# Dense weights converted in pairs of blocks, with a score tile as the integer scratch

## The chip, the core and the metric

The kernel runs on one core of a Trainium2 chip. The metric is the device time in microseconds from the launch to the end. Before the change it is 780.61 us (median of 3 runs, 776.25 to 781.67). The core's engines work side by side from queues of their own: TensorE (PE, with weight loads as PEld), VectorE (DVE), ScalarE (ACT), GpSimd (POOL), and SyncE (SP), which here only issues DMAs.

## The reference, cut to what matters

```python
# attention: 2 batches x 8 heads, 768 tokens, head size 64; a key counts for a query only in the same bucket
mask = q_bucket[:, :, :, None] == k_bucket[:, :, None, :]        # 6 sign bits of x @ proj
scores = np.where(mask, scale * q @ k.T, -1e9)
attn = softmax(scores); x = attn @ v                             # -> x: 1536 tokens x 512
# dense layer
h = x @ w_in                                                     # w_in 512 x 2048, float64
x = (h * (1 / (1 + np.exp(-1.702 * h)))) @ w_out                 # w_out 2048 x 512, float64
# mixture of 8 experts, the best 2 of a token, chosen by noisy logits
out[mask] += top2_w[mask, k, None] * (np.maximum(x[mask] @ w1[e], 0) @ w2[e])
```

The two dense weights come as float64. [...]

## The kernel before, in words

**Steps of attention.** 96 steps g go over (batch, chunk of 256 queries, pair of heads, head, half of the chunk). A step multiplies 128 queries with all 768 keys (`qk`, L269) into a score tile `s` of 128x1024 float32 in PSUM. The pool `pss` has two such tiles. `rowmax` (L281, DVE) reads the scores, writes them to SBUF as `e` and takes the row maximum; ACT forms the exponential (`expo`, L289 and L290). Steps below 24 transpose `e` on PE (L308), copy it on ACT (L316) and multiply with V in float32 (L376). Later steps split `e` into two float16 halves (`e_hi` L329, `e_lo` L338), transpose by DMA and multiply in float16 (L383). In the loop, step g issues the score product of g+2 first, then the row maximum of g+1, and last the other work due at g. `buckets` writes into the unused columns of a score tile.

**Dense layer.** After every 16 steps a chunk of 256 tokens goes through 16 parts: eight first-layer parts (`h`, L486), then two second-layer results (`px`, L497). Between them a part goes through `th` (L504, L516) and is split into `gt` (L530, L532). Afterwards routing scatters rows to a table in DRAM, and the eight experts run (L864, L895).

**Weights of the dense layer.** They come in 32 blocks of 128x512: 16 of `w_in`, then 16 of `w_out`. `w_load` issues a 512 KB DMA on SP. The raw 4 KB per partition of the first 16 blocks lies in eight regions of the still unused tiles `wo`, those of the others in `wraw`, which has three buffers. `w_bits` makes a float32 from the integer halves with three DVE instructions (L443, L446, L449); their integer tile `pfi` has one bank of PSUM of its own (tag `pb`), which only routing uses later. `w_split` scales on POOL (L462), writes the high half on ACT (L465) and the low half on POOL (L466).

**What sets the order.** PARAM holds due steps: `W` gives the step at which each block is converted, with its load due two steps ahead; `KA`, `QA`, `VA` are those of the stacked keys, queries and values, `PV` of the product with V, `ST` of the start of a chunk's dense part, `RA` of its routing, `O0` and `I0` of the DMAs that clear the output and the table. Strings choose an engine per item (`GS` for the low half of `gt`, `XN` for that of `xt`, `SC` for a scaled copy of `qsa` or `ks`, `HI` for `e_hi`). Emission in this order is a priority: up to the end of attention a scheduler with a cost model of its own fixes the queue of every engine, so instructions of neighbouring steps are interleaved. Once fixed, every engine works its queue in order, and an instruction that waits holds those behind it.

Of the kernel before, what the change touches and what calls it, by code (L numbers as in the profile page):

```python
# [57 lines left out]
PARAM = dict(GM=16, HE=lambda nm, b: 'D', OE=lambda nm, b: 'D', SC=lambda nm, b: 'D', WB=0, XO=lambda b: 'D', NG=16, WS=lambda i: 'P', TS=lambda g: True, XL=lambda g: 'D', GW=2, E0=7, T0=12, T1=16, EL=8, WX=3, PV={(1,2,3):4}, PVD=5, ST={}, VA={}, RA={}, O0=48, OS=2, IS=2, FU=16, VF=2, EC=lambda g: 'AA', QX=8, QS=3, EA=1, S1=(8,8,8,9,9,9,11,13), QE=8, XG=2, XB=2, PC=2, OH=3, BK=3, R0=18, R1=0, LK=8, WL=1, NW=3, LE=lambda nc: nc.scalar, I0=24, LQ=8, LV=0, W=[(g, 1) for g in range(-6, 30)], KA={(0,0,0):-8,(0,0,1):-6,(0,1,0):-4,(0,1,1):-2}, QA={(0,0,0):-7,(0,0,1):-3}, HI=lambda g: 'P', LO=lambda g: False)  # L58
# [20 lines left out]
PARAM.update(QA=dict(PARAM['QA']) | {(0,1,3):21,(1,2,3):84,(0,1,0):8,(0,1,1):10})  # L79

PARAM.update(KA={(0, 0, 0): -12, (0, 0, 1): -5, (0, 1, 0): -10, (0, 1, 1): -2, (0, 2, 0): -1, (0, 2, 1): 1, (0, 3, 0): 4, (0, 3, 1): 5, (1, 0, 0): 37, (1, 0, 1): 39, (1, 1, 0): 44, (1, 1, 1): 46, (1, 2, 0): 42, (1, 2, 1): 51, (1, 3, 0): 47, (1, 3, 1): 51},QA={(0, 0, 0): -15, (0, 0, 1): -4, (0, 0, 2): 1, (0, 0, 3): 3, (0, 1, 0): 8, (0, 1, 1): 10, (0, 1, 2): 16, (0, 1, 3): 21, (0, 2, 0): 24, (0, 2, 1): 28, (0, 2, 2): 30, (0, 2, 3): 33, (1, 0, 0): 38, (1, 0, 1): 41, (1, 0, 2): 47, (1, 0, 3): 52, (1, 1, 0): 57, (1, 1, 1): 56, (1, 1, 2): 61, (1, 1, 3): 69, (1, 2, 0): 72, (1, 2, 1): 69, (1, 2, 2): 80, (1, 2, 3): 84},VA={(0, 0, 0): -3, (0, 0, 1): -3, (0, 1, 0): 2, (0, 1, 1): -1, (0, 2, 0): 0, (0, 2, 1): 0, (0, 3, 0): -1, (0, 3, 1): -2, (1, 0, 0): -1, (1, 0, 1): -1, (1, 1, 0): 2, (1, 1, 1): -4, (1, 2, 0): -3, (1, 2, 1): -3, (1, 3, 0): 2, (1, 3, 1): -2},PV={(0, 0, 0): 4, (0, 0, 1): 5, (0, 0, 2): 4, (0, 0, 3): 4, (0, 1, 0): 6, (0, 1, 1): 4, (0, 1, 2): 4, (0, 1, 3): 4, (0, 2, 0): 5, (0, 2, 1): 5, (0, 2, 2): 5, (0, 2, 3): 6, (1, 0, 0): 5, (1, 0, 1): 5, (1, 0, 2): 4, (1, 0, 3): 5, (1, 1, 0): 5, (1, 1, 1): 5, (1, 1, 2): 5, (1, 1, 3): 6, (1, 2, 0): 4, (1, 2, 1): 4, (1, 2, 2): 4, (1, 2, 3): 4},RA={0: 20, 1: 20, 2: 21, 3: 21, 4: 19},ST={0: 4, 1: 4, 2: 6, 3: 4, 4: 5, 5: 3},W=[(g_,1) for g_ in [-6, -4, -3, 0, 2, 3, 4, 5, 6, 7, 7, 8, 10, 11, 12, 13, 15, 17, 17, 18, 20, 20, 20, 20, 21, 22, 22, 23, 23, 25, 25, 26]],O0=58,I0=28,GW=2,WL=2,BK=3,T0=12,T1=17,R1=2,VF=-1,OH=3,B2=2,O2=3,XS=lambda nm,b:'PPPPPP'[2*"qkv".index(nm)+b],SC=lambda nm,b:'DADD'[2*"qkv".index(nm)+b],HE=lambda nm,b:'DPDP'[2*"qkv".index(nm)+b],KC=lambda nm,b:'DDAA'[2*"qkv".index(nm)+b],QE8=lambda b:'PP'[b],GS=lambda ci,i:'PPPPPPPPPPPPPDDDDPPPDDDDDDDDPPPPPPPPPPPPPPPPPPPP'[8*ci+i],XN='P',WS=lambda i:'pppppppppppppppppppppppppppppppp'[i],EC=lambda g:2*'AAAAAAAAAAAAAAAA'[g%16],HI=lambda g:'AAAAAAAAAAAAAAAAAAAAAAAAAAAAAAAAAAAAAAAAAAAAAAAAAAAAAAAAAAAAAAAAAAAAAAAAAAAAAAAAAAAAAAAAAAAAAAAA'[g],LO=lambda g:'DPDPDPDPDPDPDPDPDPDPDDDPDDDPDPDPDDDPDDDPDDPPDDDPDDDPDDDPDDDPDDDPDDDPDDDPDDDPDDDPDDDPDDDPDDDPDDDP'[g]=="P")


@with_exitstack
def fused(ctx: ExitStack, tc: tile.TileContext, q, k, v, proj, w_in, w_out, w_gate, w_noise, noise,
          w1, w2, out, dbg=None):
# [314 lines left out]
    def pv_out(b, cc, hp):  # L401
# [19 lines left out]
    wblocks += [(wo[0][:, f], wo[1][:, f], w_out[f * 128:f * 128 + 128], SWO) for f in range(FF // 128)]
    wraw = {}

    def w_load(i):
        src = wblocks[i][2]
        if src.dtype == I64:
            if i < PARAM["WN"]:
                j = PARAM["WJ"][i % len(PARAM["WJ"])]
                x = wo[j % 2][:, 4 * (j // 2):4 * (j // 2) + 4].rearrange("p a n -> p (a n)").bitcast(I32).rearrange(
                    "p (n w) -> p n w", w=2)  # L430
            else:
                x = moe.tile([128, 512, 2], I32, name="wraw", bufs=PARAM["NW"])
            PARAM['LE'](nc).dma_start(x.rearrange("p n w -> p (n w)"), src.bitcast(I32))
        else:
            x = moe.tile([128, 512], F32, name="wraw", bufs=PARAM["NW"])
            PARAM['LE'](nc).dma_start(x, src)
        wraw[i] = x

    def w_bits(i):
        x = wraw[i]  # L440
        if wblocks[i][2].dtype == I64:
# [1 line left out]
            nc.vector.tensor_scalar(fi, x[:, :, 1], 0x07FFFFFF, 3, op0=OP.bitwise_and,  # L443
                                    op1=OP.logical_shift_left)
            yield
            nc.vector.scalar_tensor_tensor(fi, x[:, :, 1], -0x40000000, fi, op0=OP.bitwise_and,  # L446
                                           op1=OP.bitwise_or)
            yield
            nc.vector.scalar_tensor_tensor(x[:, :, 1], x[:, :, 0], 29, fi, op0=OP.logical_shift_right,  # L449
                                           op1=OP.bitwise_or)  # L450
            wraw[i] = x.bitcast(F32)[:, :, 1]

    def w_split(i):
        hi, lo, src, scale = wblocks[i]
        f, m = wraw[i], PARAM["WS"](i)
        if m == "P":
            nc.gpsimd.tensor_scalar(hi, f, scale, 1.0, op0=OP.mult, op1=OP.mult)
        elif m == "A":
            nc.scalar.activation(hi, f, AF.Copy, scale=scale)
        else:  # L460
            if m == "p":
                nc.gpsimd.tensor_scalar(f, f, scale, 1.0, op0=OP.mult, op1=OP.mult)  # L462
            else:
                nc.scalar.activation(f, f, AF.Copy, scale=scale)
            nc.scalar.activation(hi, f, AF.Copy)  # L465
            nc.gpsimd.tensor_tensor(lo, f, hi, op=OP.subtract)  # L466

    def w_rest(i):
        hi, lo, src, scale = wblocks[i]
        f = wraw.pop(i)  # L470
        if PARAM["WS"](i) in "AP":
            nc.vector.scalar_tensor_tensor(lo, f, scale, hi, op0=OP.mult, op1=OP.subtract)
# [496 lines left out]
    for b in range(B):  # L969
        for hp in range(HP):  # L970
            g = b * NCH * 16 + 4 * hp
# [9 lines left out]
        for cc in range(NCH):  # L981
            for hp in range(HP):
                g = (b * NCH + cc) * 16 + 4 * hp
# [6 lines left out]
                at(gp + 2, pv_out, b, cc, hp)  # L990
    at(min(todo) + 1, proj_parts)
    at(PARAM["GW"], gate_parts)
    wl = 0
    for g, n in PARAM["W"]:
        for _ in range(n):
            if wl < len(wblocks):
                soon(g - PARAM['WL'], w_load, wl)
                at(g, w_bits, wl)
                soon(g + 1, w_split, wl)
                at(g + 1, w_rest, wl)  # L1000
# [162 lines left out]
    with tc.If(most > CAP):  # L1163
        with tc.tile_pool(name="ov", bufs=1) as ov:
# [10 lines left out]
            x = m2.tile([128, 1024], F32, name="xo", tag="w32", bufs=8)  # L1175
            wt = [wts.tile([128, 2, 4096], F16, name=f"wo{i}", tag="w") for i in range(2)]
            nc.vector.memset(cur, 0.0)
            with tc.For_i(0, E, 1) as e:
# [5 lines left out]
                with tc.If(here > CAP):  # L1184
                    for j, (src, sw) in enumerate(((w1, SW1), (w2, SW2))):
                        for i in range(4):
                            if j == 0:
                                nc.sync.dma_start(x, src[bass.ds(e, 1), i * 128:(i + 1) * 128, :].rearrange("a p f -> (a p) f"))
                            else:
# [6 lines left out]
                                                           op1=OP.subtract)  # L1196
                    with tc.For_i(0, (OV + 127) // 128, 1) as k_:
                        with tc.If(here > k_ * 128 + CAP):
# [71 lines left out]
```

## Time and profile before

| | before |
|---|---|
| median of 3 runs | 780.61 us |
| profiled execution: time, span | 781.27 us, 779.2 us |
| mean granted TensorE clock | 0.975 of full speed |
| busy PE / DVE / ACT / POOL | 703.3 / 495.6 / 445.0 / 282.6 us |
| DMA moved | 136.83 MB, mean 176 GB/s |

The span runs from the first to the last instruction; 2.1 us of the profiled execution's time lie around it. Busy time is a sum over the whole span, while the kernel has stages with different limits, so the views by stretch and the waits say more than the sums. In every row times are in us unless marked ns; `out<-in` are the program's names and L is a line of the kernel before.

### The profile page before, as it was taken

To read this page: it belongs to the slowest core of one execution; us is meant where nothing else is said; L and a number is where in the kernel's file an instruction comes from. 1 tells how busy PE (TensorE), PEld (TensorE's weight loads), DVE (VectorE), ACT (ScalarE), POOL (GpSimd) and SP (SyncE) were. 2 spreads that over 40 slices of the span, in tenths; PEclk is the share of its full clock that TensorE was granted. 3 is DMA by queue.
4 is the path that set the end of the run, shared out by engine and by line. 5 is a ranking of instruction groups with operands and counts; after the bars stand their busy time and mean duration, and the time that the engine had idled before them with its cause. 6 is when DMAs were issued, how large, how long until landed. Compare 5 with 4: busy or idle time off the path is not lost.

```text
span 779.2 us, 14900 instructions
## 1 busy us (share of the span) xinstructions
PE 703.3 (90%) x5432; PEld 433.1 (56%) x5433; DVE 495.6 (64%) x1249; ACT 445.0 (57%) x958; POOL 282.6 (36%) x356
## 2 busy tenths in 40 slices
PE   1767599999988989999999999899999999999995
PEld 0444366647844765577577575556554545545452
DVE  7789979857786687687778417565543635445220
ACT  3768877758876686678668334344442635335220
POOL 7555956853466144106032323241021130312203
PEclk9979699999999999999999999999999999999998
DMA  8999476999989999965785750849987768584213
GB/s 196 234 253 330 141 199 169 295 248 194 180 186 217 183 221 221 186 137 101 130 195 110 151 210 10 248 137 240 270 159 196 217 102 262 84 233 86 28 18 45
DMA packets 254973, 136.83 MB, mean 176 GB/s; under 512 B 211696, under 2 KB 230704, under 8 KB 254896
## 3 DMA queue, kind: packets, MB, share of 16 engines
q1 hardware_dynamic: 248880, 122.68, 65.4%
q0 software_dynamic: 6016, 13.16, 9.6%
q8 instruction: 43, 0.70, 0.4%
q14 instruction: 34, 0.28, 0.1%
HBM read 62.27 MB, written 23.20 MB: 110 GB/s over the span
## 4 chain that ended last, share of the span: by engine, by line
PE 37%; DVE 5%; DMA 4%; ACT 2%; issue 2%; POOL 1%; POOLq 0%; DVEq 0%; ACTq 0%
PE ph L864 16%; PE py L895 14%; PE px L497 3%; PE h L486 2%; DMA et<-er 1%; PE py L889 1%; DMA xg<-slots 1%; DVE er L338 1%; DMA slots<-xr,si 1%; ACT er L329 1%; POOL slots L746 1%; PE pv L383 1%; ACT e L290 1%; POOL out_dram L912 1%; DVE e L281 1%
## 5 line engine op out<-in xcount | busy, mean ns | idle before, releaser
L486 PE MATMUL h<-xt,wi 128*128 128x256 f16 x1152 | 136.0, 275 | 3.0 <-DVE th L516 2.9
L864 PE MATMUL ph<-xg,ew 128*128 128x400 f16 (+2 forms) x864 | 132.6, 314 | 4.7 <-DMA xg<-slots 3.9
L497 PE MATMUL px<-wo,gt 128*128 128x512 f16 x576 | 132.4, 382 | 1.3 <-DVE th L516 1.3
L804 DVE SCALAR_TENSOR_TENSOR ew<-w,ew 128x1024 f16<-128x1024 f32 x64 | 77.8, 1225 | 84.0 <-ACT ew L803 83.6
L912 POOL DMA_INDIRECT out_dram<-yo,ti x32 | 54.0, 1687 | 201.4 <-ACT yo L905 195.7
L895 PE MATMUL py<-ew,ht 128*128 128x512 f16 x576 | 126.0, 379 | 0.0
L486 PEld LDWEIGHTS <-wi 128*128 128x128 f16 x1152 | 111.7, 98 | 21.7 <-issue 4.8
L269 PE MATMUL s<-kt,qt 76*128 76x512 f16 (+3 forms) x384 | 87.2, 349 | 27.0 <-DVE e L281 21.3
L864 PEld LDWEIGHTS <-ew 128*128 128x128 f16 x864 | 80.4, 98 | 54.7 <-issue 6.7
L895 PEld LDWEIGHTS <-ht 128*128 128x128 f16 x576 | 56.1, 98 | 66.9 <-issue 0.2
L281 DVE TENSOR_SCALAR_CACHE_REDUCE e<-s 128x768 f32<-128x768 f32 x96 | 90.7, 948 | 2.2 <-PE pt L308 0.8
L497 PEld LDWEIGHTS <-gt 128*128 128x128 f16 x576 | 55.3, 98 | 65.4 <-issue 4.2
L338 DVE SCALAR_TENSOR_TENSOR er<-e,mx,er 128x768 f16<-128x768 f32 x68 | 71.2, 1049 | 31.4 <-ACT er L329 30.9
L290 ACT ACTIVATE e<-e,mx 128x768 f32<-128x768 f32 x96 | 89.4, 932 | 1.8
L329 ACT ACTIVATE er<-e,mx 128x768 f16<-128x768 f32 x68 | 62.9, 929 | 37.4 <-DMA et<-er 34.6
L532 POOL TENSOR_TENSOR gt<-th,gt 128x512 f16<-128x512 f32 x36 | 44.8, 1245 | 103.0 <-ACT gt L530 102.8
L905 ACT ACTIVATE yo<-py,wv 128x512 f32<-128x512 f32 x24 | 16.5, 688 | 94.6 <-PE py L895 57.9
L269 PEld LDWEIGHTS <-qt 76*128 76x128 f16 (+1 forms) x384 | 35.9, 102 | 57.1 <-DVE e L281 18.3
L874 ACT ACTIVATE ht<-ph 128x400 f16<-128x400 f32 (+2 forms) x72 | 33.5, 466 | 58.9 <-PE ph L864 58.1
L803 ACT ACTIVATE ew<-w 128x1024 f16<-128x1024 f32 x64 | 66.3, 1048 | 0.1
L875 DVE SCALAR_TENSOR_TENSOR ht<-ph,ht 128x400 f16<-128x400 f32 (+2 forms) x72 | 37.5, 523 | 30.9 <-ACT ht L874 30.8
L383 PE MATMUL pv<-et,vt 128*64 128x256 f16 x648 | 44.4, 279 | 3.1 <-DMA et<-er 3.1
(235 smaller groups left out, 930.1 us busy)
## 6 DMA issues: line engine op xcount, KB each, us to landing
w<-in_moe_w_dram SPq DMA_DIRECT2D x64, 512.0 KB, 5.9
wo<-in_moe_w_in_dram SPq DMA_DIRECT2D x16, 512.0 KB, 5.4
wraw<-in_moe_w_out_dram SPq DMA_DIRECT2D x16, 512.0 KB, 4.4
slots<-blank SPq DMA_DIRECT2D x6, 1032.0 KB, 8.5
v<-in_v_dram SPq DMA_DIRECT2D x28, 192.0 KB, 3.8
out_dram<-zeros SPq DMA_DIRECT2D x13, 256.0 KB, 3.5
q<-in_q_dram SPq DMA_DIRECT2D x24, 128.0 KB, 3.1
k<-in_k_dram SPq DMA_DIRECT2D x16, 192.0 KB, 3.1
```

Of the source, the lines that this page charges most:

```text
L269: nc.tensor.matmul(ps[:, n0 * 128:n1 * 128], qt[:kr, s, h, t, :], kt[:kr, s, h, n0:n1, :].rearrange("p c t -> p (c t)"), start=(s == 0), s ...
L281: nc.vector.tensor_scalar(e32, st[g]["ps"][:, :S], -FAR, -TOP, op0=OP.max, op1=OP.max, accum_out=mx[:, 0:1])
L290: nc.scalar.activation(e32, e32, AF.Exp, scale=0.125, bias=st[g]["mx"][:, 1:2], accum_out=sms[b, cc, hp][:, 2 * h + t:2 * h + t + 1] if g ...
L329: nc.scalar.activation(er[:, 0], st[g]["e"], AF.Copy, scale=r)
L338: nc.vector.scalar_tensor_tensor(er[:, 1], d["e"], d["mx"][:, 3:4], er[:, 0], op0=OP.mult, op1=OP.subtract)
L486: nc.tensor.matmul(ph[:, a, :], wi[ws][:, d, f0:f0 + 128], xt[:, d, xs, :], start=(d == 0 and ws == 0 and xs == 0), stop=(d == HP - 1 and ...
L497: nc.tensor.matmul(px, gts[ci, f // 2][:, gs, f % 2, t * 128:t * 128 + 128], wo[ws][:, f, :], start=(f == 0 and gs == 0 and ws == 0), stop ...
L803: nc.scalar.activation(hi, x, AF.Copy, scale=SW1 if j == 0 else SW2)
L804: nc.vector.scalar_tensor_tensor(lo, x, SW1 if j == 0 else SW2, hi, op0=OP.mult, op1=OP.subtract)
L864: nc.tensor.matmul(ph[:, :c1 - c0], w[:, ws, d * FE + f * 128:d * FE + f * 128 + 128], xg[e, p][:, xs * HP + d, :], start=(d == 0 and ws = ...
L895: nc.tensor.matmul(py, ht[:, f, hs, t * 128:t * 128 + 128], w[:, ws, f * DM:(f + 1) * DM], start=(i == 0), stop=(i == n - 1))
L912: ins = nc.gpsimd.indirect_dma_start(out=dst, out_offset=bass.IndirectOffsetOnAxis(ap=ti[:np_, o:o + 1], axis=0), in_=yo[:np_, :nd], in_of ...
```

## The change

Blocks 0 to 23 are now handled as 12 pairs. Both blocks of a pair are loaded into one region of 8 KB per partition, of which the `wo` tiles hold four (`WJ` names the region of each pair: 0,1,2,3,0,1,2,3,2,3,2,3; blocks 24 to 31 write their results into regions 2 and 3). `w_bits` and `w_split` then run once for a pair, on 128x1024. The integer tile of a pair is taken from the pool of the two score tiles; blocks 24 to 31 keep the tile `pb` and the buffers `wraw`. A load into a region is due no earlier than the step after the conversion that frees it, and a conversion no earlier than the step after its load. `w_rest`, the variants of `w_split` by `WS`, and `WS` itself are no longer used.

```diff
+PARAM.update(WP=24,WJ=(0,1,2,3,0,1,2,3,2,3,2,3))
...
+    WP = PARAM["WP"]
+    wpairs = [(wi[0][:, d:d + 2, f:f + 512], wi[1][:, d:d + 2, f:f + 512])
+              for f in range(0, FF, 512) for d in range(0, HP, 2)]
+    wpairs += [tuple(w[:, f:f + 2].rearrange("p a n -> p (a n)") for w in wo) for f in range(0, FF // 128, 2)]
...
+        if i >= WP or w == 1:
+            x = moe.tile([128, 512, w], I32 if w == 2 else F32, name="wraw", bufs=PARAM["NW"])
+            wraw[i] = x
+            h = 0
+        else:
+            h = i % 2
+            if h == 0:
+                j = PARAM["WJ"][i // 2]
+                wraw[i] = wo[j % 2][:, 8 * (j // 2):8 * (j // 2) + 8].rearrange("p a n -> p (a n)").bitcast(
+                    I32).rearrange("p (n w) -> p n w", w=2)
+            x = wraw[i - h]
+        x = x[:, 512 * h:512 * h + 512].rearrange("p n w -> p (n w)")
+        PARAM['LE'](nc).dma_start(x, src.bitcast(I32) if w == 2 else src)
...
+        if i < WP:
+            fi = pss.tile([128, 1024], F32, name="pfi", tag="s").bitcast(I32)
+        else:
             fi = psr.tile([128, 512], I32, name="pfi", tag="pb", bufs=1)
...
+        f, scale = wraw.pop(i), wblocks[i][3]
+        nc.gpsimd.tensor_scalar(f, f, scale, 1.0, op0=OP.mult, op1=OP.mult)
+        if i < WP and wblocks[i][2].dtype == I64:
+            hi, lo = wpairs[i // 2]
+            if i < 16:
+                f = f.rearrange("p (a n) -> p a n", a=2)
+        else:
+            hi, lo = wblocks[i][:2]
+        nc.scalar.activation(hi, f, AF.Copy)
+        nc.gpsimd.tensor_tensor(lo, f, hi, op=OP.subtract)
...
+                gl, r = g - PARAM['WL'], None
+                if wl < WP and wblocks[wl][2].dtype == I64:
+                    r = PARAM["WJ"][wl // 2]
+                    gl = max(gl, free_at.get(r, gl))
+                    g = max(g, gl + 1)
+                    if wl % 2:
+                        free_at[r] = g + 1
+                soon(gl, w_load, wl)
+                if wl >= WP or wblocks[wl][2].dtype != I64:
+                    at(g, w_bits, wl)
+                    soon(g + 1, w_split, wl)
+                elif wl % 2:
+                    at(g, w_bits, wl - 1)
+                    soon(g + 1, w_split, wl - 1)
```

The due steps and the engines are set anew in the same change. `W` is now [-6,-4,-3,0,2,3,4,5,6,7,7,8,10,11,12,12,13,17,17,18,18,18,18,19,20,22,22,23,23,25,25,28], so the 12 pairs are converted at steps -4, 0, 3, 5, 7, 8, 11, 12, 17, 18, 19 and 20. These also change:

- Keys: (0,0,1) from -5 to -10, (0,1,0) -10 to -7, (0,2,1) 1 to 2, (0,3,1) 5 to 4, (1,1,1) 46 to 45.
- Queries: (0,0,0) from -15 to -14, (0,1,0) 8 to 5, (0,2,0) 24 to 25, (1,1,2) 61 to 62. Five entries of the values' `VA` move by one step.
- Product with V: (0,0,0) from 4 to 5, (0,0,1) 5 to 7, (0,1,0) 6 to 5, (1,0,0) 5 to 7, (1,1,1) 5 to 7 steps after the unit's first.
- Chunk 1 of the dense layer starts two steps later (`ST` 4 to 6); the routing of chunks 1, 2 and 3 moves from 20, 21, 21 to 23, 18, 20; `O0` goes from 58 to 57 and `I0` from 28 to 27.
- Engines: `XN` moves the low halves of `xt` of the first seven units (L414) from POOL to DVE. `GS` moves that of `gt` (L532) from POOL to DVE for three parts of chunk 0 and four of chunk 1. `SC` moves L170 for the eight key tiles of batch 1 from DVE to ACT. `HI` moves `e_hi` (L329) of steps 43 to 48 from ACT to POOL. Other entries of the strings that changed are not read.

## Rows read from the trace of the kernel before

**Rows 1.** Busy time by stretch: span, then busy us (instructions) of each engine, clock, DMA.

```profile
20.00:160.00 140.00, 111.99 (x842) 71.29 (x839) 119.55 (x257) 104.88 (x262) 93.94 (x111) 0.91 0.88 231
160.00:500.00 340.00, 319.57 (x2706) 213.00 (x2704) 238.81 (x666) 224.89 (x509) 114.38 (x121) 0.98 0.79 169
500.00:779.00 279.00, 267.86 (x1842) 146.54 (x1840) 121.83 (x280) 108.64 (x171) 59.45 (x71) 0.99 0.65 154
40.00:60.00 20.00, 14.10 (x116) 8.53 (x114) 16.89 (x38) 12.66 (x35) 9.94 (x12) 0.74 1.10 259
80.00:100.00 20.00, 12.08 (x61) 6.57 (x60) 16.36 (x30) 15.59 (x40) 17.17 (x22) 0.66 0.51 141
```

**Rows 2.** What PE waited for, 20 to 160 us: total us, times, longest.

```profile
PE s L269 <- DVE e L281: 13.5, 7, 5.5
PE pt L308 <- ACT et L316: 3.8, 9, 0.7
PE pt L308 <- ACT e L290: 3.2, 5, 0.8
```

**Rows 3.** The two longest of these waits, and DVE's queue ahead of the second.

```profile
48.28 0.82 PE L269 MATMUL s<-kt,qt 128*128 128x512 f16 x2 [5.07 <-DVE e L281]
...
77.73 0.68 DVE L443 TENSOR_SCALAR pfi<-wo 128x512 int32<-128x512 int32 x1
...
84.67 0.94 DVE L281 TENSOR_SCALAR_CACHE_REDUCE e<-s 128x768 f32<-128x768 f32 x1
...
85.68 2.74 PE L269 MATMUL s<-kt,qt 128*128 128x512 f16 x8 [5.48 <-DVE e L281]
```

**Rows 4.** Groups of instructions: busy us, mean ns, idle before them.

```profile
L446 DVE SCALAR_TENSOR_TENSOR pfi<-wraw,pfi 128x512 int32<-128x512 int32 x16 | 11.0, 690 | 0.2
L804 DVE SCALAR_TENSOR_TENSOR ew<-w,ew 128x1024 f16<-128x1024 f32 x64 | 77.8, 1225 | 84.0 <-ACT ew L803 83.6 <-SPq L1163 0.4
L281 DVE TENSOR_SCALAR_CACHE_REDUCE e<-s 128x768 f32<-128x768 f32 x96 | 90.7, 948 | 2.2 <-PE pt L308 0.8
L269 PE MATMUL s<-kt,qt 76*128 76x512 f16 (+3 forms) x384 | 87.2, 349 | 27.0 <-DVE e L281 21.3
L465 ACT ACTIVATE wo<-wraw 128x512 f16<-128x512 f32 x16 | 10.7, 667 | 3.8 <-POOL wraw L462 3.8
L803 ACT ACTIVATE ew<-w 128x1024 f16<-128x1024 f32 x64 | 66.3, 1048 | 0.1
L462 POOL TENSOR_SCALAR wo<-wo 128x512 f32<-128x512 f32 x16 | 10.7, 667 | 14.0 <-DVE wo L449 9.0 <-DVE sm L353 3.9 <-DVE r L359 0.7
L466 POOL TENSOR_TENSOR wi<-wo,wi 128x512 f16<-128x512 f32 x16 | 18.8, 1173 | 4.9 <-ACT wi L465 4.1 <-ACT mx L289 0.8
L399 DVE TENSOR_TENSOR xn<-pv,xn 128x256 f32<-128x256 f32 x7 | 2.9, 413 | 3.5 <-ACT xn L392 3.5
L414 POOL TENSOR_TENSOR xt<-xn,xt 128x256 f16<-128x256 f32 x7 | 4.8, 681 | 6.9 <-ACT xt L412 6.9
L532 POOL TENSOR_TENSOR gt<-th,gt 128x512 f16<-128x512 f32 x36 | 44.8, 1245 | 103.0 <-ACT gt L530 102.8
L532 DVE TENSOR_TENSOR gt<-th,gt 128x512 f16<-128x512 f32 x12 | 8.2, 684 | 0.4 <-ACT gt L530 0.3
L170 DVE TENSOR_SCALAR ks<-ks 128x384 f16<-128x384 f16 x16 | 5.6, 353 | 8.0 <-POOL ks L162 8.0
L329 ACT ACTIVATE er<-e,mx 128x768 f16<-128x768 f32 x68 | 62.9, 929 | 37.4 <-DMA et<-er 34.6 <-DVE er L338 1.1 <-DVE mx L295 0.8
```

**Rows 5.** All row maxima from 20 to 160 us (two instructions each).

```profile
20.00:160.00 140.00, 29.52 (x62) 0.91 0.88 231
```

**Rows 6.** DMA issues of the page: count, KB each, us to landing.

```profile
wo<-in_moe_w_in_dram SPq DMA_DIRECT2D x16, 512.0 KB, 5.4
...
slots<-blank SPq DMA_DIRECT2D x6, 1032.0 KB, 8.5
```

**Rows 7.** DVE's waits over the whole span, the line of the weights' loads.

```profile
DVE pfi L443 <- DMA wo<-in_moe_w_in_dram: 6.0, 5, 1.8
```

More of the change, by code (lines that the diff above doesn't have):

```diff
@@ L66 @@
 PARAM.update(FU=24,WS=lambda i:'p')
-PARAM.update(WN=16,WJ=(0,1,2,3,4,5,6,7))
+PARAM.update(WN=16,WJ=(0,1,2,3))
 PARAM.update(W=[(g_,1) for g_ in [-6,-4,-2,0,2,3,4,5,7,8,9,10,12,13,14,15,17,18,19,20,20,21,21,22,22,23,23,24,24,25,25,26]])
@@ L425, in w_load @@
         src = wblocks[i][2]
[L426 to L433, printed above, removed]
-        else:
-            x = moe.tile([128, 512], F32, name="wraw", bufs=PARAM["NW"])
-            PARAM['LE'](nc).dma_start(x, src)
@@ L437, in w_load @@
-        wraw[i] = x
+        w = 2 if src.dtype == I64 else 1
+        if i >= WP or w == 1:
+            x = moe.tile([128, 512, w], I32 if w == 2 else F32, name="wraw", bufs=PARAM["NW"])
+            wraw[i] = x
+            h = 0
+        else:
+            h = i % 2
[4 more added lines that the diff above has]
+            x = wraw[i - h]
@@ L439, in w_bits @@
+        x = x[:, 512 * h:512 * h + 512].rearrange("p n w -> p (n w)")
+        PARAM['LE'](nc).dma_start(x, src.bitcast(I32) if w == 2 else src)
     def w_bits(i):
         x = wraw[i]
-        if wblocks[i][2].dtype == I64:
-            fi = psr.tile([128, 512], I32, name="pfi", tag="pb", bufs=1)
[L443 to L451, printed above, removed]
@@ L453, in w_split @@
-    def w_split(i):
[L454 to L459, printed above, removed]
-        else:
[L461 to L472, printed above, removed]
+        if wblocks[i][2].dtype != I64:
+            wraw[i] = x[:, :, 0]
+            return
+        if i < WP:
+            fi = pss.tile([128, 1024], F32, name="pfi", tag="s").bitcast(I32)
+        else:
+            fi = psr.tile([128, 512], I32, name="pfi", tag="pb", bufs=1)
+        nc.vector.tensor_scalar(fi, x[:, :, 1], 0x07FFFFFF, 3, op0=OP.bitwise_and,
+                                op1=OP.logical_shift_left)
@@ new lines, in w_bits @@
+        yield
+        nc.vector.scalar_tensor_tensor(fi, x[:, :, 1], -0x40000000, fi, op0=OP.bitwise_and,
+                                       op1=OP.bitwise_or)
+        yield
+        nc.vector.scalar_tensor_tensor(x[:, :, 1], x[:, :, 0], 29, fi, op0=OP.logical_shift_right,
+                                       op1=OP.bitwise_or)
+        wraw[i] = x.bitcast(F32)[:, :, 1]
+    def w_split(i):
+        f, scale = wraw.pop(i), wblocks[i][3]
[4 more added lines that the diff above has]
+                f = f.rearrange("p (a n) -> p a n", a=2)
+        else:
+            hi, lo = wblocks[i][:2]
+        nc.scalar.activation(hi, f, AF.Copy)
+        nc.gpsimd.tensor_tensor(lo, f, hi, op=OP.subtract)
@@ L992, in fused @@
     at(PARAM["GW"], gate_parts)
-    wl = 0
+    wl, free_at = 0, {}
     for g, n in PARAM["W"]:
@@ L996, in fused @@
             if wl < len(wblocks):
[L997 to L1000, printed above, removed]
+                gl, r = g - PARAM['WL'], None
[12 more added lines that the diff above has]
+                    soon(g + 1, w_split, wl - 1)
                 wl += 1
```

1 line of the change is left out of this document (added).

## The prediction, made before the result was known

> **What bounds the kernel now.** I read the busy time by stretch first, then the waits of PE in the stretch that the change touches, then the two longest of them with DVE's queue in front of them, and last the groups of instructions for prices. From 500 us on, PE is busy 267.9 of 279 us with the experts; nothing of the change lies there. From 160 to 500 us it is busy 319.6 of 340 us. From 20 to 160 us, where all but the first weights are converted, it idles 140 − 112.0 = 28.0 us, while DVE works 119.6 of 140 us (85%), ACT 104.9 and POOL 93.9 [rows 1]. After 160 us PE has little slack, so what the front saves or loses reaches the end nearly whole.
>
> In the front PE waits above all for row maxima: a score product can't start before DVE has read the tile that it will overwrite. That is 13.5 us in 7 waits; ACT, at the transposes of `e`, holds PE for 7.0 us [rows 2]. Two of the waits, 5.07 and 5.48 us, make 10.6 us. Ahead of the second one, DVE works through seven conversion instructions and small work for the query stacks, from 77.73 to 84.67 us, before the row maximum that PE needs [rows 3]. So DVE isn't only full there; its order is bad at these places. In the two stretches of 20 us that hold these waits the granted clock is 0.74 and 0.66 [rows 1], between the levels of 1.2 and 2.4 GHz, and the falls come after PE sat idle for 5 us.
>
> **The change, part by part.** The profiled execution took 781.3 us, 0.7 above the median of the three runs; the sum is made against it.
>
> 1. Pairs on DVE. Before: 24 x 3 instructions at 0.690 = 49.7 us. For 128x1024 I take the 1.225 us of L804, which has this size and two inputs: 12 x 3 x 1.225 = 44.1 us, so **−5.6 us**. The row maximum of 768 columns out of a score tile takes 0.948 us [rows 4]; the line through 0.690 at 512 and this gives 1.21, so an operand in PSUM is no dearer. The other bound is twice 0.690, a saving of nothing.
>
> 2. Pairs on ACT and POOL. ACT: 24 x 0.667 − 12 x 1.048 = 3.4 us less, or nothing if length scales. POOL has no row of 1024; between twice a block (no saving) and ACT's proportion it saves 0 to 9. I take 3 [rows 4].
>
> 3. Work moved to DVE in the front. The seven low halves of `xt` cost about 0.413 each (L399, same shape): +2.9 us on DVE, −4.8 on POOL. Three low halves of `gt` of chunk 0 cost 0.684 instead of 1.245: +2.1 on DVE, −3.7 on POOL [rows 4]. DVE's net in the front is therefore −5.6 + 2.9 + 2.1 = **−0.6 us**: the retimed engines spend what pairing saves, and it is POOL that gets lighter, by about 11.5 of 93.9 us. That shortens the way from `th` to `gt` and the weights' last split. POOL is on no long wait of PE directly, so I take **−2 us** (0 to −4.5). ACT's 3.4 us meet the 7.0 us for which PE waits on it: **−1.5 us** (0 to −3.4).
>
> 4. The score tile as scratch. While a pair is converted, one of the two score tiles is held for three DVE instructions, 3.7 us. The next score product then has to wait for the row maximum of the product just before it, so look-ahead falls from two products to one. Eleven of the twelve pairs come when score products run. There are 62/2 = 31 row maxima in 140 us [rows 5], a step of 4.5 us; PE's share of a step is 112/31 = 3.6 us, of which the score product takes 4 x 0.349 = 1.4 [rows 4]. If the three instructions stand right before the row maximum, PE has 2.2 us of other work against 3.7 + 0.95 = 4.6 us: a wait of 2.4 us, 26 us over eleven pairs. If they stand elsewhere, it is nothing, since DVE has other work to do and PE slack to spend. The nearest rows are 7 waits of this kind in 31 steps, 13.5 us, so most steps pass without one; I take **+2.2 us**, 0.2 a pair, and keep 0 and 26 for the range.
>
> 5. New due times. They place every queue's instructions anew, so the two long waits needn't come back. Both arise from conversions queued ahead of a due row maximum, and nothing in the rows ties them to a dependency. I take half: **−5.3 us** (0 to −10.6). With them goes part of the slow clock: PE's 26.2 busy us in those two stretches [rows 1] would be 14.1 x 0.74 + 12.1 x 0.66 = 18.4 at full clock, 7.8 less, mostly where PE isn't the limit: **−1.5 us** (0 to −3.9, half).
>
> 6. Loads. Bytes, count and queue (SP) stay. A region of a pair is free only after its conversion, so the pairs at steps 19 and 20 are loaded one step, 4.5 us, ahead, and landing takes 5.4 us [rows 6]. DVE waited 6.0 us for such loads before [rows 7]. What stands behind a waiting conversion are row maxima. I take **+1 us** (0 to +5.4). Clearing the table and the output one step earlier moves 6 and 13 DMAs on SP; beside the transposes of keys and probabilities they are hidden, and one that wasn't would cost its 8.5 us of landing once [rows 6].
>
> 7. Later steps, 160 to 500 us. Four more `gt` halves go to DVE (4 x 0.684), eight scaled key copies leave it (8 x 0.353): nothing in sum. Six `e_hi` leave ACT (6 x 0.929) for POOL at between 1.5 x 0.667 and 1.5 x 1.173 us each [rows 4]; a step separates them from `e_lo`, and POOL is busy a third of that time [rows 1]. Without that step of cover it is 6 x 0.8 us. Chunk 1 of the dense layer starts two steps later, with the same PE work. Of 20.4 us of idle PE I take **−1 us** (+5 to −4).
>
> Sum: −0.6 − 2 − 1.5 + 2.2 − 5.3 − 1.5 + 1 − 1 = −8.7 us: 772.6 for an execution like the profiled one, 0.7 less at the median: **772 us**.
>
> **A rule that speaks against it.** The Trainium skill, page Perfetto Trace Analysis, section Optimizing Scalar/DVE Operations, says that where VectorE isn't saturated but leaves bubbles on other engines, breaking instructions up may get work done sooner; joining them is the reverse. For a saturated engine the same section advises grouping. The rows give DVE 85% in the front with 13.5 us of waits on PE, so both halves could apply. By the first, the sum would come out as the third rival below.
>
> **The rivals.**
>
> - *Both long waits go* (0.14): parts 5, 3 and 2 at their good ends, nothing for part 4: 781.3 − 0.7 − 0.6 − 10.6 − 3.9 − 3 = about 762 us. For it: the waits are accidents of order. Against it: a new order has accidents of its own.
> - *No change* (0.28): the waits move and keep their size, DVE's −0.6 is all that is left, with a little of part 3: about 779 us. For it: DVE's work in the front hardly falls, and DVE is the fullest engine beside PE.
> - *Longer instructions in the way* (0.08): a row maximum that comes due behind a conversion waits for up to 1.22 − 0.69 = 0.53 us more. With one in most of the 20 steps that hold pairs, half of that each is +5.3 us, and without gains elsewhere about 785 us.
> - *Slower: the missing score tile decides* (0.20). Place: the score product after each conversion. It decides where the conversion stands before the row maximum in DVE's queue, as seven conversion instructions did in [rows 3]. At half of its 26 us, less 3 us of parts 2 and 3: 781.3 − 0.7 + 13 − 3 = about 791 us. Against it: PE's idle fifth in the front can take up part of it.
>
> **How the numbers follow.** My forecast (0.30) is the likeliest case. I call a change of over 1% (below 772.8 or above 788.4 us) measurable. Forecast and first rival make faster 0.44; no change and most of the third rival make same 0.34; the slower rival and the rest of the third make slower 0.22. The range leaves out the far part of the two outer cases, about a tenth each: 757 to 792 us; the forecast alone would be 764 to 780.
>
> **What will show it.** Part 1: 36 instructions of 128x1024 near 1.22 us; at 1.38 it was wrong. Parts 2 and 3: POOL's busy time from 20 to 160 us near 82 us, DVE's within 2 us of 119. Part 4: PE's waits for row maxima, with the ones after conversions longer than 2 us if it decides. Part 5: no PE wait of 5 us between 20 and 160 us, and the clock of all 20 us stretches near 1. Part 6: DVE's wait for the weights' loads above 7 us if I was too kind. The prediction is wrong in its core if PE's idle time in the front is not some 6 us smaller, or if the end moves without the front.

## The result and the profile after

The changed kernel takes 788.34 us (median of 7 runs, 785.1 to 793.28) against 781.44 us of the kernel before, run beside it on the same chip: a ratio of 1.0107, 95% interval 1.0069 to 1.0145. It is slower by 1.1%, where 772 us were forecast. The profiled executions took 791.3 and 781.3 us, so the traces show some 10 us of loss where the medians show 6.9. The profiles of two experiments, e3 and e4, fell into disturbed executions; of these two only medians and ratios are used.

**Where the time went.** The busy time by stretch, columns as in [rows 1]; the last line but one and the last are two of the 20 us stretches:

```profile
20.00:160.00 140.00, 107.93 (x774) 72.87 (x773) 123.40 (x220) 99.92 (x241) 78.11 (x72) 0.82 0.80 219
160.00:500.00 340.00, 321.03 (x2719) 213.94 (x2719) 238.76 (x671) 224.54 (x517) 120.12 (x128) 0.99 0.78 168
...
60.00:80.00 20.00, 14.52 (x77) 8.79 (x74) 16.60 (x29) 12.14 (x31) 7.73 (x7) 0.67 1.06 342
80.00:100.00 20.00, 15.12 (x90) 9.55 (x88) 19.97 (x35) 17.20 (x42) 13.60 (x15) 0.67 0.54 166
```

From 20 to 160 us PE idles 32.1 us instead of 28.0 [rows 1] and gets 774 matmuls done instead of 842, at a clock of 0.82 instead of 0.91. The row maxima come in the order of the steps, so they make a common ruler for two traces. It measures attention alone: between two steps PE also does other work, and an order can put that off. The row maximum of step 21 starts at 112.41 us instead of 105.50, 6.9 us late, that of step 31 is 7.6 us late, and the last, of step 95, 9.9 us. So most of the loss is made in the front, where the prediction expected gains. These are the two rows of step 21, before and after:

```profile
105.50 0.96 DVE L281 TENSOR_SCALAR_CACHE_REDUCE e<-s 128x768 f32<-128x768 f32 x1
```

```profile
112.41 0.95 DVE L284 TENSOR_SCALAR_CACHE_REDUCE e<-s 128x768 f32<-128x768 f32 x1
```

By the last row maximum nearly the same number of matmuls is done, so there the lag can be split. These are the stretches up to it, of the kernel before, of the changed kernel and of e2 below, which has the new due steps and engines without the pairs:

```profile
0.00:432.12 432.12, 371.51 (x3150) 247.11 (x3152) 343.24 (x890) 312.84 (x744) 201.53 (x264) 0.96 0.87 196
0.00:442.00 442.00, 376.19 (x3139) 253.19 (x3141) 348.32 (x856) 307.85 (x730) 190.23 (x230) 0.93 0.84 191
0.00:441.81 441.81, 380.16 (x3139) 251.83 (x3141) 343.05 (x892) 308.91 (x742) 195.06 (x254) 0.93 0.85 191
```

Of the changed kernel's 9.9 us, 5.2 are more idle time of PE (65.8 instead of 60.6) and 4.7 are more busy time for the same work. In e2 it is 1.0 and 8.6.

**What PE waited for**, 20 to 160 us, columns as in [rows 2]; L272 is the score product, L284 the row maximum, L311 the transposes of `e`, L293 the exponential, L463 the last conversion instruction of a pair:

```profile
PE s L272 <- DVE e L284: 10.9, 6, 4.5
PE pt L311 <- ACT e L293: 7.2, 5, 3.2
PE s L272 <- DVE wo L463: 3.2, 3, 2.2
...
PE pt L311 <- ACT et L319: 0.9, 3, 0.4
```

The waits for row maxima fell a little, 13.5 to 10.9 us, and the two of over 5 us [rows 3] are gone. PE waits longer at the transposes for the exponential, 7.2 instead of 3.2 us [rows 2], and there is a new kind: a score product that waits until a pair has let go of its score tile. One such case in DVE's queue and PE's, from the timeline (start, duration):

```profile
63.09 1.23 DVE L457 TENSOR_SCALAR pfi<-wo 128x1024 int32<-128x1024 int32 x1
64.36 1.23 DVE L460 SCALAR_TENSOR_TENSOR pfi<-wo,pfi 128x1024 int32<-128x1024 int32 x1
65.87 1.94 DVE L165 TENSOR_SCALAR qsb<-q 128x256 f16<-128x256 f32 x1 [0.28 <-DMA q<-in_q_dram]
67.73 0.41 DVE L402 TENSOR_TENSOR xn<-pv,xn 128x256 f32<-128x256 f32 x1
68.06 1.21 DVE L463 SCALAR_TENSOR_TENSOR wo<-wo,pfi 128x1024 int32<-128x1024 int32 x1
...
69.33 0.98 PE L272 MATMUL s<-kt,qt 128*128 128x512 f16 x4 [2.24 <-DVE wo L463]
```

The scheduler puts other work between the three instructions, so the tile is held for 6.2 us here, and over the twelve pairs for 3.8 to 7.3 us, 5.0 in the mean, where the prediction had 3.7. When it is free, PE starts at once.

The longer waits at the transposes are for the most part not seen to come from a held tile. The longest of them, 3.2 of the 7.2 us, in DVE's, ACT's and PE's queues:

```profile
36.32 0.29 DVE L165 TENSOR_SCALAR qsb<-q 128x256 f16<-128x256 f32 x1 [1.57 <-DMA q<-in_q_dram]
...
37.37 2.24 DVE L219 TENSOR_TENSOR ks<-pc 128x36 f16<-128x36 f32 x2
39.53 0.95 DVE L284 TENSOR_SCALAR_CACHE_REDUCE e<-s 128x768 f32<-128x768 f32 x1
...
41.00 0.92 ACT L293 ACTIVATE e<-e,mx 128x768 f32<-128x768 f32 x1
...
42.07 1.54 PE L311 MATMUL pt<-ident,e 128*128 128x128 f32 x6 [3.20 <-ACT e L293]
```

The row maximum stands behind a query stack, for whose load DVE waits, and behind a key stack; the pair before had let go of its tile at 32.6 us.

**The priced instructions**, by line and shape, columns as in [rows 4]:

```profile
L457 DVE TENSOR_SCALAR pfi<-wo 128x1024 int32<-128x1024 int32 x12 | 15.1, 1255 | 3.2 <-DMA wo<-in_moe_w_out_dram 3.0
L463 DVE SCALAR_TENSOR_TENSOR wo<-wo,pfi 128x1024 int32<-128x1024 int32 x12 | 14.7, 1227 | 0.1
L460 DVE SCALAR_TENSOR_TENSOR pfi<-wo,pfi 128x1024 int32<-128x1024 int32 x12 | 14.7, 1225 | 0.1
L469 POOL TENSOR_SCALAR wo<-wo 128x1024 f32<-128x1024 f32 x12 | 13.9, 1155 | 8.9 <-DVE wo L463 6.2 <-DVE sm L358 1.2 <-DVE r L362 0.9
L476 ACT ACTIVATE wi<-wo 128x1024 f16<-128x1024 f32 x8 | 9.6, 1203 | 1.1 <-POOL wo L469 1.1
L477 POOL TENSOR_TENSOR wi<-wo,wi 128x1024 f16<-128x1024 f32 x8 | 17.0, 2128 | 10.9 <-ACT wi L476 5.5 <-ACT mx L292 5.4
L417 DVE TENSOR_TENSOR xt<-xn,xt 128x256 f16<-128x256 f32 x7 | 3.3, 466 | 0.2 <-ACT xt L415 0.2
```

The DVE instructions came out at their price, those of ACT at 1.203 instead of 1.048 us, and none of the paired ones costs more than the two that it replaced.

### The profile page after: what moved, and what is told of

Its sections match the earlier page's. It is cut to its first block, busy times and chain, and to the rows that moved or that the text cites. A ratio compares the mean times of both kernels' runs of the same rounds, so it can differ in the third digit from the quotient of the medians.

```text
span 789.7 us, 14792 instructions
## 1 busy us (share of the span) xinstructions
PE 710.1 (90%) x5432; PEld 440.3 (56%) x5433; DVE 501.0 (63%) x1219; ACT 442.1 (56%) x948; POOL 268.6 (34%) x324
## 4 chain that ended last, share of the span: by engine, by line
PE 46%; DVE 15%; DMA 10%; ACT 6%; issue 5%; POOL 4%; SPq 1%; POOLq 0%; DVEq 0%; ACTq 0%
PE ph L869 15%; PE py L900 14%; PE px L502 6%; PE h L491 5%; DMA et<-er 5%; DVE er L341 4%; DVE e L284 3%; ACT er L332 2%; PE pv L386 2%; PE s L272 2%; PE py L894 2%; ACT e L293 1%; POOL slots L751 1%; DMA slots<-xr,si 1%; DMA qt<-qsb 1%
## 5 line engine op out<-in xcount | busy, mean ns | idle before, releaser
L491 PE MATMUL h<-xt,wi 128*128 128x256 f16 x1152 | 141.1, 280 | 5.5 <-DVE th L521 5.5
L502 PE MATMUL px<-wo,gt 128*128 128x512 f16 x576 | 130.2, 379 | 1.3 <-DVE th L521 1.3
L491 PEld LDWEIGHTS <-wi 128*128 128x128 f16 x1152 | 113.6, 100 | 28.9 <-issue 9.1
L917 POOL DMA_INDIRECT out_dram<-yo,ti x32 | 50.1, 1566 | 204.3 <-ACT yo L910 196.3
L272 PE MATMUL s<-kt,qt 128*128 128x512 f16 (+3 forms) x384 | 86.1, 351 | 23.9 <-DVE e L284 15.1
L284 DVE TENSOR_SCALAR_CACHE_REDUCE e<-s 128x768 f32<-128x768 f32 x96 | 90.7, 950 | 6.5 <-PE pt L311 4.3
L293 ACT ACTIVATE e<-e,mx 128x768 f32<-128x768 f32 x96 | 89.4, 932 | 1.7
L332 ACT ACTIVATE er<-e,mx 128x768 f16<-128x768 f32 x62 | 57.4, 929 | 23.5 <-DMA et<-er 20.4
L537 POOL TENSOR_TENSOR gt<-th,gt 128x512 f16<-128x512 f32 x29 | 34.7, 1196 | 101.7 <-ACT gt L535 101.6
L272 PEld LDWEIGHTS <-qt 76*128 76x128 f16 (+1 forms) x384 | 37.1, 103 | 53.3 <-issue 22.4
```

Of the source, the lines that this page charges most:

```text
L272: nc.tensor.matmul(ps[:, n0 * 128:n1 * 128], qt[:kr, s, h, t, :], kt[:kr, s, h, n0:n1, :].rearrange("p c t -> p (c t)"), start=(s == 0), s ...
L284: nc.vector.tensor_scalar(e32, st[g]["ps"][:, :S], -FAR, -TOP, op0=OP.max, op1=OP.max, accum_out=mx[:, 0:1])
L293: nc.scalar.activation(e32, e32, AF.Exp, scale=0.125, bias=st[g]["mx"][:, 1:2], accum_out=sms[b, cc, hp][:, 2 * h + t:2 * h + t + 1] if g ...
L332: nc.scalar.activation(er[:, 0], st[g]["e"], AF.Copy, scale=r)
L491: nc.tensor.matmul(ph[:, a, :], wi[ws][:, d, f0:f0 + 128], xt[:, d, xs, :], start=(d == 0 and ws == 0 and xs == 0), stop=(d == HP - 1 and ...
L502: nc.tensor.matmul(px, gts[ci, f // 2][:, gs, f % 2, t * 128:t * 128 + 128], wo[ws][:, f, :], start=(f == 0 and gs == 0 and ws == 0), stop ...
```

## The experiments

The ratio of each is to the kernel before, measured beside it in the same session, with its 95% interval. Three theories stood against each other at first: that borrowing the score tile costs, that the new settings (due steps and engines) cost, and that longer instructions hold up row maxima. "Lag" is how late the row maximum of step 21 starts in its trace against 105.50 us.

| | kernel | us | ratio (interval) | lag |
|---|---|---|---|---|
| | changed kernel | 788.3 | 1.0107 (1.0069 to 1.0145) | 6.9 |
| e1 | pairs, old settings | 787.3 | 1.0110 (1.0071 to 1.0149) | 6.6 |
| e2 | single blocks, new settings | 789.5 | 1.0119 (1.0076 to 1.0162) | 4.2 |
| e3 | before, score tile as scratch | 791.1 | 1.0128 (1.0089 to 1.0168) | |
| e4 | changed, halves in own bank | 789.8 | 1.0118 (1.0060 to 1.0177) | |
| e5 | before, one block later | 792.7 | 1.0146 (1.0084 to 1.0208) | 1.1 |
| e6 | before, one query earlier | 783.1 | 1.0029 (0.9991 to 1.0067) | -1.4 |
| e7 | before, `xt` on DVE | 787.3 | 1.0079 (1.0045 to 1.0112) | 3.8 |
| e8 | before, clearing earlier | 788.0 | 1.0110 (1.0039 to 1.0182) | -0.2 |
| e9 | changed, one pair later | 801.0 | 1.0244 (1.0197 to 1.0292) | 11.6 |
| e10 | changed, one query back | 793.0 | 1.0151 (1.0110 to 1.0192) | 9.4 |
| e11 | changed, clearing back | 794.7 | 1.0153 (1.0096 to 1.0211) | 8.2 |
| e12 | changed, `xt` back on POOL | 800.1 | 1.0247 (1.0205 to 1.0290) | 9.9 |
| e13 | e9, halves in own bank | 788.3 | 1.0129 (1.0081 to 1.0176) | 6.3 |
| e14 | e10, halves in own bank | 782.9 | 1.0041 (1.0014 to 1.0069) | 1.7 |
| e15 | e12, halves in own bank | 792.9 | 1.0181 (1.0137 to 1.0224) | 5.3 |
| e16 | e5, score tile as scratch | 793.4 | 1.0177 (1.0133 to 1.0221) | 10.3 |
| e17 | e6, score tile as scratch | 795.5 | 1.0153 (1.0078 to 1.0228) | 8.1 |
| e18 | e7, score tile as scratch | 796.8 | 1.0193 (1.0100 to 1.0286) | 7.0 |

### The parts of the change, one at a time (e1 to e4)

e1 leaves out the new settings, the last added line of PARAM, and keeps the pairs.

> Pairs, regions and score tile as in the change, all due steps and engines as before it. Score-tile theory: the loss of 7 us is in this part, so 786 to 791 us. Settings theory (the new due steps and engines cost it): 778 to 783 us. If 36 fewer instructions on DVE count for anything it could fall to 776.

e2 adds that line to the kernel before, with its regions and its split unchanged.

> Single blocks with the integer tile of before, with the new due steps and engines. Settings theory: 786 to 791 us, with the slow clock from 60 to 100 us as in the changed kernel. Score-tile theory: 777 to 783 us.

e3 changes only where the integer tile lies:

```diff
-            fi = psr.tile([128, 512], I32, name="pfi", tag="pb", bufs=1)
+            if i < 24:
+                fi = pss.tile([128, 1024], F32, name="pfi", tag="s").bitcast(I32)[:, :512]
+            else:
+                fi = psr.tile([128, 512], I32, name="pfi", tag="pb", bufs=1)
```

> The kernel before, but the integer tile of blocks 0 to 23 (128x512, still one block at a time) is taken from the two score tiles. Score-tile theory: about twice as many takings, each with 2.1 us of instructions instead of 3.7: 786 to 795 us, the loss before 160 us. Settings theory and long-instruction theory: 780 to 783 us.

e4 is the changed kernel with the conversion of a pair in two halves, in the bank that had it before:

```diff
-        if i < WP:
-            fi = pss.tile([128, 1024], F32, name="pfi", tag="s").bitcast(I32)
-        else:
+        for xx in ([x[:, :512], x[:, 512:]] if i < WP else [x]):
             fi = psr.tile([128, 512], I32, name="pfi", tag="pb", bufs=1)
...
```

> The changed kernel, but the integer conversion of a pair runs in two halves of 128x512 through the bank of its own; loads, scaling and splits stay paired. Score-tile theory: back to 779 to 784 us in spite of 5.6 us more work on DVE. Settings theory: 788 to 793 us. Long-instruction theory: also 780 to 784 us, so this run alone doesn't part it from the score tile; e3 does.

All four came out at 1.011 to 1.013. The parts don't add up to the whole; each alone costs as much as all of them. No theory expected that of e1 and e2 together, and e4 should have been fast under the score-tile theory: for the changed kernel itself, giving the score tile back gained nothing. What the four have in common is that each gives the scheduler a new problem, and so gets queues in a new order. That made another theory, of order.

### New orders of the same work (e5 to e8)

Each of these is put behind the last PARAM line of the kernel before:

```diff
+PARAM.update(W=[(g+(i==8),n) for i,(g,n) in enumerate(PARAM['W'])])   # e5
+PARAM.update(QA=dict(PARAM['QA'])|{(0,1,0):7})                        # e6
+PARAM.update(XN='D')                                                  # e7
+PARAM.update(O0=57,I0=27)                                             # e8
```

> The kernel before with one number changed: block 8 is due at step 7 instead of 6. No work is added or removed, but the scheduler lays out PE's, DVE's and ACT's queues anew from there on. Order theory (e1 to e4 all cost 1.1% because each made the scheduler form a new order, and the one before was an unusually good one): 783 to 792 us. Score-tile, settings and long-instruction theories: 779 to 782 us.

> The kernel before with one query stack due one step earlier (step 7 instead of 8): a small change of order in the front, no change of work. Order theory: 780 to 788 us, less than e5. The other theories: 779 to 782 us.

> The kernel before with the low halves of xt on DVE instead of POOL, seven instructions of 0.41 us, one of the new settings. Order theory: 783 to 792 us. If only the work counts: 2.9 us more on DVE, 780 to 784 us.

> The kernel before with the DMAs that clear the table and the output due one step earlier, two of the new settings. The order up to about step 26 stays; behind it all queues change. Order theory, as a matter of the front: 780 to 784 us; if an order behind step 26 matters as much: 783 to 790 us. The other theories: 779 to 782 us.

e5 and e8 settle it for order as a cause: no instruction is added, lengthened or moved to another engine, and they cost 1.46% and 1.10%. e6 displaces fewest instructions of the four and costs least, 0.3%, not separable from nothing. e8 leaves the front alone (lag -0.2 us) and loses behind step 26, so an order is worth as much there. e5 shows the same from another side. At step 31 it is 2.8 us ahead of the kernel before, with 896 matmuls done instead of 928, so that the lead is work put off; at step 95 it is 10.6 us behind. Up to there PE idled 6.7 us more than before and was busy 3.9 us longer; in e8 it idled 4.8 us more and was busy as long as before (371.7 us). The two rows of e5, to be held against 163.29 and 432.12 us before:

```profile
160.46 0.94 DVE L281 TENSOR_SCALAR_CACHE_REDUCE e<-s 128x768 f32<-128x768 f32 x1
...
442.70 0.95 DVE L281 TENSOR_SCALAR_CACHE_REDUCE e<-s 128x768 f32<-128x768 f32 x1
```

PE's waits of e5 from 160 to 500 us are many small ones; the first of these lines was 3.1 us before, the second 1.5 and the third 1.3:

```profile
PE pv L383 <- DMA et<-er: 5.5, 3, 2.8
PE h L486 <- DVE th L516: 3.4, 5, 2.1
PE px L497 <- DVE th L516: 2.9, 2, 1.7
```

### New orders of the changed kernel (e9 to e12)

Each of these is put behind the last PARAM line of the changed kernel:

```diff
+PARAM.update(W=[(g+(i in (9,)),n) for i,(g,n) in enumerate(PARAM['W'])])   # e9
+PARAM.update(QA=dict(PARAM['QA'])|{(0,1,0):8})                             # e10
+PARAM.update(O0=58,I0=28)                                                  # e11
+PARAM.update(XN='P')                                                       # e12
```

> The changed kernel with one number moved: the fifth pair is due at step 8 instead of 7. Order theory: the changed kernel is one draw of many, this is another with the same work, anywhere from 781 to 794 us. Score-tile theory (a loss that pairs bring whatever the order): 786 to 791 us.

> The changed kernel with one query stack back at step 8 instead of 5. Order theory: another draw, 781 to 794 us. If that setting as such were to blame: 780 to 783 us.

> The changed kernel with the clearing DMAs back at their old steps; the front keeps its order, all after step 26 is laid out anew. In the kernel before the opposite edit cost 1.1%. If early clearing as such costs: 3 to 8 us less than the changed kernel, 780 to 785 us. Order theory: no such gain is due, 784 to 794 us.

> The changed kernel with the low halves of xt back on POOL, 2.9 us less on DVE. In the kernel before the opposite edit cost 0.8%. If these instructions on DVE as such cost: 780 to 785 us. Order theory: another draw, 781 to 794 us, with no gain due.

e11 and e12 undo settings whose introduction cost 1.1% and 0.8% in the kernel before, and here undoing them costs too: it wasn't the settings as such. e9, e11 and e12 came out above the 794 us that the order theory allowed. The level is another one, too. One-number edits of the kernel before cost 0.3 to 1.5%, a mean of 0.9%; one-number edits of the changed kernel stand 1.5 to 2.5% above the kernel before, a mean of 2.0%. Order alone gives no reason for that, so it seemed that pairs cost something beside it. e1 doesn't fit in: it has pairs with the old settings and stands at 1.1%.

### The score tile in the same settings (e13 to e18)

e13, e14 and e15 are e9, e10 and e12 with the edit of e4; e16, e17 and e18 are e5, e6 and e7 with the edit of e3.

> e9 (fifth pair a step later), but the integer conversion in two halves through the bank of its own, as in e4. By step 21 the six kernels with pairs stand 6.6 to 11.6 us behind the kernel before, those with single blocks -1.4 to 4.2. Structure theory (long instructions on a score tile cost some 6 us of the front in any order): 5 to 12 us below e9's 801. Order theory alone: no sign is due, 788 to 802 us.

> e10 (query stack back), with the conversion in halves through the bank of its own. Structure theory: 783 to 789 us against e10's 793. Order theory alone: 785 to 801 us, either sign against e10.

> e12 (xt on POOL), with the conversion in halves through the bank of its own. Structure theory: 787 to 794 us against e12's 800. Order theory alone: either sign against e12.

> e5 (block 8 a step later), with the integer tile of blocks 0 to 23 taken from the score tiles as in e3, still 128x512. If it is the score tile that costs, and not the length: 3 to 10 us above e5's 792.7. If the length: within the draw, 783 to 794 us.

> e6 (a query stack a step earlier), with the integer tile of blocks 0 to 23 from the score tiles, 128x512. If the score tile costs: 786 to 795 us against e6's 783.1. If the length: the draw of a new order, 781 to 790 us.

> e7 (xt on DVE), with the integer tile of blocks 0 to 23 from the score tiles, 128x512. If the score tile costs: 790 to 798 us against e7's 787.3. If the length: either sign against e7, 782 to 792 us.

Taking the score tile away and halving the length: e9 to e13 -1.1%, e10 to e14 -1.1%, e12 to e15 -0.7%, the changed kernel to e4 +0.1%; a mean of -0.7%, or 5.5 us, although DVE has 5.6 us more to do. Adding the score tile at the old length: e5 to e16 +0.3%, e6 to e17 +1.2%, e7 to e18 +1.1%, the kernel before to e3 +1.3%; a mean of +1.0%, or 7.7 us. Seven of eight have the sign that the score tile asks for. e13 to e15 came out in the ranges that this theory gave or just better, e17 and e18 in theirs or just above; e16, 0.8 us above e5 where 3 to 10 were expected, missed. Two of the eight start from the kernels before and after: e3's 1.3% says little, as new orders of the kernel before cost 1.0% in the mean without any score tile, and e4's says that for the changed kernel the tile's price didn't show. The other six all have the sign, with a mean of 0.9%, some 7 us. Length isn't in the second set at all, so it isn't needed. Each of the eight also has a new order, so a single difference proves little. PE's waits from 20 to 160 us in e6 and then in e17, the same settings without and with the score tile:

```profile
PE s L269 <- DVE e L281: 9.7, 8, 3.8
...
PE pt L308 <- ACT e L290: 2.1, 4, 0.9
```

```profile
PE s L269 <- DVE e L281: 10.2, 7, 2.2
PE pt L308 <- ACT e L290: 7.7, 5, 3.7
PE s L269 <- DVE wo L452: 3.7, 2, 2.0
...
PE s L269 <- DVE wraw L452: 1.3, 1, 1.3
```

And e10 and e14, the same settings with the score tile and without it:

```profile
PE pt L311 <- ACT e L293: 9.6, 7, 3.3
PE s L272 <- DVE e L284: 8.2, 7, 4.5
PE s L272 <- DVE wo L463: 2.6, 2, 1.3
```

```profile
PE s L272 <- DVE e L284: 7.5, 9, 1.7
PE s L272 <- ACT qsb L226: 3.6, 1, 3.6
PE pt L311 <- ACT e L293: 3.5, 7, 0.8
```

Each time the score tile brings the waits for a conversion, 5.0 and 2.6 us, and the transposes' wait for the exponential is longer by 5.6 and 6.1 us. In these two pairs the waits for row maxima hardly move; from e9 to e13 and from e7 to e18 they are 5.5 and 6.0 us shorter with the tile. Over all traces the transposes' line reads 7.2 to 10.7 us in the nine kernels that use a score tile as scratch, and 1.2 to 4.6 us in the nine that don't, the kernel before among them. The lag at step 21 parts them too, 6.6 to 11.6 against -1.4 to 6.3 us; that at step 31 does so less well, since e1 is then 2.5 us ahead and e2, without the tile, 11.3 us behind.

These nine are not nine independent cases. In eight of them (all but e1) one wait at the transposes, at 41 to 44 us, makes 3.2 to 5.0 us of the line, and in DVE's queue the row maximum stands there behind a query stack: after a wait for its load of 5.6 to 6.3 us in e16 to e18, of 1.6 to 2.0 us in the changed kernel and e9 to e12. Without this one wait the eight read 2.9 to 6.6 us, which overlaps the others. So the conversions' waits, 2.5 to 5.2 us in each of the nine, are the part that the traces tie to the held tile. The rest goes with it in two orders of the front, one of e16 to e18 and one of the other five, and whether the tile or the order makes it isn't shown.

No kernel of these beats the kernel before. e14 comes nearest among those that keep the paired loads and splits, at 1.0041.

## Why the prediction was wrong

**The step that failed is part 5**, the new due times. It took it that a new order would on the average drop half of the two long waits, 5.3 us, and that nothing could be lost there. The two long waits did go, and PE's idle time in the front still rose, by 4.1 us, where a fall of some 6 us had been named as the sign. The new due steps and engines alone, without pairs, cost 1.2% (e2), some 9 us. New orders without a score tile as scratch cost 0.3 to 1.5% (e2, e5 to e8), a mean of 1.0% or 7.6 us. The order before isn't an average one that happens to have two bad places; against the neighbours that were run it is a good one. The first rival, which made even more of these waits, fell with it. The clock's term in part 5, 1.5 us of gain, had the wrong sign too, as shown below.

**Part 4 was mis-sized**, as far as the comparisons go. The sum took 2.2 us; the six comparisons of nudged kernels give some 7 us in the mean, while e4 gives nothing for the changed kernel itself. The direct wait for a held tile is 3.2 us in the changed kernel, near the 2.2 taken, although the tile is held for 5.0 instead of 3.7 us, since other work is laid between the three instructions. Where the rest of the price is made stays open. The rival on the score tile was right in its direction, and its 791 us are close in part by luck: it put half of 26 us at the tile and nothing at the order, and the runs show less for the tile and a loss by order beside it.

The two together would be 1.7 to 2.0%, which is where the neighbours of the changed kernel stand. The changed kernel itself stands at 1.07%, and so does e1 with the old settings, at 1.10%. Against e1 the new settings gained nothing, against the kernel before they cost 1.2%. How the 1.07% divides between order and score tile isn't shown; the parts don't add.

**Part 1** was right to the hundredth: 1.225, 1.227 and 1.255 us against 1.225, the last with one instance of 1.52 in it. **Part 2**: POOL saves 12 x (2 x 0.667 + 2 x 1.173 - 1.155 - 2.128) = 4.8 us where 3 was taken, ACT, at 1.203 us for eight pairs and 1.131 for four, 24 x 0.667 - 14.1 = 1.9 instead of 3.4. The gain of 1.5 us at PE's waits on ACT didn't come: at the transposes they went from 7.0 to 8.1 us. **Part 3**: 7 x 0.466 = 3.3 us on DVE, 2.9 predicted; POOL's 78.1 us in the front is even below the 82 named, DVE's 123.4 above the 117 to 121. That POOL's relief brought a gain can't be seen; POOL was on none of PE's long waits. **Part 6** was too dark: DVE waited 3.0 us for the pairs' loads, all of `w_out`, less than the 6.0 of [rows 7]. **Part 7** can't be told apart: PE idles 19.0 us from 160 to 500 us, 1.4 less than before, but the lag grows by 2.3 us from step 31 to step 95.

The sentence that what the front saves or loses reaches the end nearly whole is half right. The changed kernel's loss does, 7.6 us at step 31 and 9.9 at step 95. But e5 and e8, not behind at step 31, lost 10.6 and 5.0 us by step 95: PE's 20 us of idle time after 160 us can grow.

**The clock.** The prediction named a clock near 1 in all 20 us stretches. It was 0.67 from 60 to 80 and from 80 to 100 us, after waits of PE, and 0.82 over the front instead of 0.91. It is a part of the loss: the 144 transposes of the front took 364 ns each instead of 311, and up to step 95 PE was busy 4.7 us longer for the same work. In e2, as late as the changed kernel, nearly all is busy time at a lower clock, 8.6 us, with 1.0 us more idle time. It isn't needed for a loss: e9, with e12 the slowest of all, has 0.91 over the front, as the kernel before, and e8 lost 5.0 us with PE as long busy as before. The transposes in the front, before and after (total us, mean ns):

```profile
L308 PE MATMUL pt<-ident,e 128*128 128x128 f32 x144 | 25.8, 311 | 7.2 <-ACT et L316 3.8 <-ACT e L290 3.2
```

```profile
L311 PE MATMUL pt<-ident,e 128*128 128x128 f32 x144 | 30.6, 364 | 8.0 <-ACT e L293 7.2 <-ACT et L319 0.9
```

What the clock alone costs no run here separates from the order that brings it.

**The page's rule**, from the Trainium skill, Perfetto Trace Analysis, Optimizing Scalar/DVE Operations, that breaking instructions up may help: its sign is seen in e13 to e15, but these also free the score tile, and e16 to e18 show the loss with instructions of the old length. No run here shows length alone to cost anything. The same page's section Identifying Performance Opportunities says that repeated bubbles on the engine that should be saturated can mean that SBUF or PSUM is lacking for the next tile. The traces agree in part: PE's waits for a tile held by a conversion make 2.5 to 5.2 us in the nine kernels that lend a score tile.

**What stays open.** How much the length of the instructions matters by itself, what in a given order makes it good, and by which way the score tile costs more than its direct waits. A run of both variants in one and the same fixed order would settle the score tile's price better than differences of draws; that wasn't tried.

## What to carry to other kernels

Where a scheduler lays out the queues anew for every edit, an edit's effect is its own cost plus a draw from the orders: here one or two changed due steps of the same work cost 0.3 to 1.5% (e5, e6, e8). Before a gain of a few us is put down to an edit, give the kernel before and the kernel after the same few neutral nudges and compare the two groups. See in the traces, too, whether the nudged kernels differ at the place in question: here eight of nine shared one long wait. And split a lag into idle and busy time of the engine that bounds the kernel before looking for a wait: in e2 PE waited hardly longer than before.

## What the runs showed of the hardware

Nothing contradicted the rows. A DVE instruction that reads or writes integers in a score tile in PSUM runs at the pace of one in SBUF: 1.225 us for 128x1024, as L804 in [rows 4]. Of TensorE's clock the traces show what it costs a given instruction: a float32 transpose of 128x128 in the front took 311 ns in the mean where the granted clock was 0.91, and 364 ns where it was 0.82.
